# A fixed instruction order for every engine, a spatial product with k outermost, and the middle column inside the odd transform products

## Chip, cores and metric

The kernel runs on one core of one Trainium2 chip. Times are device microseconds (us) from the first to the last instruction of one execution; a kernel's time is the median of its runs.

## The reference

```python
# x: 8 x 3072 x 256, w_in: 256 x 1024, w_spatial: 3072 x 3072, w_out: 512 x 256
X = np.fft.fft(np.fft.fft(x, axis=1), axis=2).real
h = np.maximum(X @ w_in, 0.0)
u, v = h[..., :512], h[..., 512:]
v_n = (v - mean(v)) / np.sqrt(var(v) + 1e-06)            # over the last axis
v_s = np.einsum('ts,bsd->btd', w_spatial, v_n) + b_spatial[None, :, None]
out = (u * v_s) @ w_out
```

The transform over the last axis is folded into `w_in`. The transform over the sequence is done by symmetry: x is added to and subtracted from its reversed copy ("folds"), and the halves are multiplied with cosine and sine tables. Most of the work is the spatial product, 3072 x 3072 by 3072 x 512, eight times (once a batch). In batch 0 the kernel also turns `w_spatial`: 96 pieces are loaded, cast to bf16 by GpSimd, transposed by TensorE, copied out and stored; from batch 1 on the turned weights are loaded again from memory.

Words used below: k numbers the 24 blocks of 128 rows over which one spatial sum runs, and "bank" stands for the PSUM tile of 128 x 512 in which the kernel gathers one such sum. The folds leave two columns without a partner, 0 and 128: their copies are the "edges", and column 128 alone is the "middle column". Four rows of x, one in each quarter, are the "special row" and have a fold of their own. A "settled batch" is one of batches 1 to 6.

## The kernel before

```python
    def turn_w(wt):                                    # batch 0 only, 96 pieces
        wb = wbpool.tile([P, WCOL], BF16, name="wb", tag="wb")       # 2 buffers
        nc.gpsimd.tensor_copy(out=wb, in_=wr)          # or with columns reversed
        load_w()
        pt = psM.tile([P, GK, P], BF16, name="pt", tag="psM")
        for kk in range(GK):
            nc.tensor.transpose(pt[:, kk, :], wb[:, 128 * kk:128 * kk + 128], ident)
        # ... copied to wt by VectorE or ScalarE in turn, and stored

    def dct_class(b, c, gx, sp, eo):                   # c = 0..3
        # ... pe: 3 (c even) or 6 (c odd) products of 384 columns, + the special row
        ops_e += [(xe[:, 0:128], ctx_[:, c, 0:n])]     # 4 rows
        # ... po_: 3 or 6 products, and for odd c the special row again
        nc.scalar.copy(out=view(eo, c, [[4, n]]), in_=pe[:, 0:n])
        nc.vector.tensor_scalar(out=view(eo, EOW + c, [[4, n]]), in0=po_[:, 0:n], ...)

    def dct_128(b, gx, sp, eo):                        # the middle column: one output row
        for c in range(4):
            # ... 3 or 6 products with lhsT of one column, + the special row
        for c in range(4):
            nc.scalar.copy(out=view(eo, EOW + c, [[4, n]])[0:1], in_=pm[32 * c:32 * c + 1, 0:n])

    def spatial(b, c, dt, v, wts, ut):                 # k innermost, two PSUM banks
        pw = psW.tile([P, TC], FP32, name="pw", tag="psW")
        for k in range(KT):
            nc.tensor.matmul(pw, lhsT=v[:, k, 128 * dt:128 * dt + 128],
                             rhs=wts[k // GK][:, k % GK, :], start=(k == 0), stop=(k == KT - 1))
        tm = tpool.tile([P, TC], FP32, name="tm", tag="tm")
        nc.vector.tensor_tensor(out=tm, in0=pw, in1=bbc[:, TC * c:TC * c + TC], op=ALU.add)
        gt = gpool.tile([P, TC], BF16, name="gt", tag="gt")
        nc.vector.tensor_tensor(out=gt, in0=tm, in1=ut, op=ALU.mult)
        return gt

    for b in range(B):                                 # the order is left to the scheduler
        for c in range(NCH):                           # 6 column blocks of 512
            uts = [u_tile(b, c, dt, cur["eo"]) for dt in range(NDT)]
            for dt in range(NDT):
                gts.append(spatial(b, c, dt, cur["v"], wts[c], uts[dt]))
                # ... after dt 0 the projection of the block before; turn_w or loads of
                # weights; one step of the next batch's folds, transform and v
```

## Time and profile before

| | before |
|---|---|
| time, median of the first 3 runs | 1539.09 us (1534.65 to 1540.53) |
| TensorE busy | 1408 us, 91% |
| end of batch 0 (start of its last gate addition) | 374.9 us |
| batches 1 to 6, each, same mark | 168.05 to 169.3 us |
| batch 7, same mark | 145.2 us, and 7 us to the end |

A "gate" is the addition of the bias to a finished spatial sum and the product with u; the last addition of a batch is a mark. The prediction counts with another mark, the first spatial product of batch 1: in before that is 376.6 us, 1.7 after the gate mark. The prediction shows the page's lines on busy engines, slices and waits. First, lines of TensorE's waits in the window from 100 to 400 us (total, times, longest, all in us):

```profile
PE pt L154 <- POOL wb L149: 6.2, 10, 0.8
PE pt L154 <- POOL wb L146: 6.1, 10, 1.3
```

In the kernel before, TensorE's transposes wait 12 us for GpSimd's casts after 100 us, in twenty short waits. Lines of the order of time: start, duration, engine, operation, and in brackets the idle time before it and what ended that.

```profile
126.85 1.23 DVE L308 TENSOR_TENSOR sm<-xt 128x1024 f32<-128x1024 f32 x1 [1.91 <-DMA xt<-xr]
...
151.08 1.23 DVE L308 TENSOR_TENSOR sm<-xt 128x1024 f32<-128x1024 f32 x1 [10.97 <-DMA xt<-xr]
...
156.45 1.89 PE L469 MATMUL pw<-wt,v_t 128*128 128x512 bf16 x4 [15.26 <-ACT v_t L445]
```

VectorE stands in front of batch 1's folds for 1.9 and 11.0 us; the normalised v of batch 0 is behind the second one, and TensorE waits 15.3 us for it.

### The profile page before, as it was taken

What the parts mean: (1) busy time and instruction counts of PE and PEld (TensorE: products, weight loads), DVE (VectorE), ACT (ScalarE), POOL (GpSimd) and SP (SyncE); (2) the same over time, 40 slices, a digit from 0 to 9 for tenths busy, and PEclk for the clock granted to TensorE, in tenths of its full rate; (3) what the DMA queues carried; (4) which work ended last, traced back from release to release, by engine and by line L of the source; (5) the groups of instructions that cost most, each with busy time, mean ns of one, the idle gap of its engine ahead of it and who ended that gap; (6) DMA issues with size and microseconds to landing.
All of it is one profiled execution on the core that took longest, in us unless ns stands there. A gap on an engine that the chain in (4) does not pass through costs nothing.

```text
span 1539.1 us, 18367 instructions
## 1 busy us (share of the span) xinstructions
PE 1408.1 (91%) x7107; PEld 677.9 (44%) x7244; DVE 709.0 (46%) x1466; ACT 479.3 (31%) x806; POOL 143.1 (9%) x202
## 2 busy tenths in 40 slices
PE   1363799999999999999999999999999999999998
PEld 0121444444444444444444444444444444444444
DVE  4755633764247523663248523753256422452222
ACT  3242433444134421342134412432134313341111
POOL 2811342440000000000000000000000000000000
PEclk9566899999999999999999999999999999999999
DMA  7564887884336242453434432633433433324331
GB/s 239 175 244 149 276 292 247 288 302 153 115 123 236 96 181 107 156 200 110 178 129 159 155 132 96 230 139 137 151 124 137 151 128 126 130 106 182 139 149 69
DMA packets 100232, 255.31 MB, mean 166 GB/s; under 512 B 13200, under 2 KB 59824, under 8 KB 100016
## 3 DMA queue, kind: packets, MB, share of 16 engines
q1 hardware_dynamic: 64912, 215.54, 39.6%
q10 hardware_dynamic: 26112, 25.17, 4.6%
q0 software_dynamic: 9120, 13.42, 2.6%
q8 instruction: 56, 0.92, 0.2%
q14 instruction: 32, 0.26, 0.1%
HBM read 210.80 MB, written 56.62 MB: 174 GB/s over the span
## 4 chain that ended last, share of the span: by engine, by line
PE 81%; DMA 8%; DVE 6%; POOL 3%; ACT 1%; issue 1%; SPq 0%; another core or an unknown queue 0%; POOLq 0%; ACTq 0%; DVEq 0%
PE pw L469 59%; PE po L485 5%; DMA xt<-xr 5%; PE pu L461 5%; PE pv L435 4%; PE pm L409 2%; PE pe L386 2%; DMA xr<-in_x_dram 2%; PE pt L154 2%; DVE stt L439 1%; DVE sm L308 1%; DVE xt L310 1%; POOL wb L146 1%; DMA x<-xr 1%; POOL wb L149 1%
## 5 line engine op out<-in xcount | busy, mean ns | idle before, releaser
L469 PE MATMUL pw<-wt,v_t 128*128 128x512 bf16 x4494 | 1023.0, 380 | 40.9 <-ACT v_t L445 35.3
L469 PEld LDWEIGHTS <-v_t 128*128 128x128 bf16 x4608 | 448.5, 98 | 570.3 <-ACT v_t L445 41.4
L473 DVE TENSOR_TENSOR tm<-pw,bbc 128x512 f32<-128x512 f32 x192 | 132.6, 691 | 610.2 <-PE pw L469 610.2
L463 ACT ACTIVATE ut<-pu 128x512 bf16<-128x512 f32 x192 | 101.3, 606 | 186.7 <-PE pu L461 182.3
L476 DVE TENSOR_TENSOR gt<-tm,ut 128x512 bf16<-128x512 f32 x192 | 135.1, 704 | 13.2 <-DVE tm L473 0.5
L439 DVE BATCH_NORM_STATS2 stt<-r 128x6 f32<-128x512 f32 x192 | 125.1, 681 | 29.9 <-ACT r L438 29.8
L489 ACT COPY ot<-po 128x512 f32<-128x512 f32 x96 | 56.2, 585 | 253.8 <-PE po L485 251.0
L438 ACT ACTIVATE r<-pv 128x512 f32<-128x512 f32 x192 | 106.9, 595 | 85.8 <-PE pv L435 73.2
L435 PE MATMUL pv<-weo,eo_t 128*128 128x512 bf16 x278 | 88.6, 394 | 7.0 <-ACT eo_t L413 3.1
L445 ACT ACTIVATE v_t<-r,rs 128x512 bf16<-128x512 f32 x96 | 78.1, 813 | 49.0 <-DVE rs L443 45.9
L485 PE MATMUL po<-wob,gt 128*128 128x256 bf16 x768 | 91.9, 273 | 0.9 <-DVE gt L476 0.9
L461 PE MATMUL pu<-eo_t,weo 128*128 128x512 bf16 x282 | 81.8, 379 | 3.8 <-ACT r L438 2.6
L485 PEld LDWEIGHTS <-gt 128*128 128x128 bf16 x768 | 75.0, 98 | 20.1 <-DVE gt L476 1.2
L388 ACT CAST eo_t<-pe 128x384 bf16<-128x384 f32 (+1 forms) x32 | 32.6, 1019 | 159.3 <-PE pe L386 159.2
L154 PE MATMUL pt<-ident,wb 128*128 128x128 bf16 x576 | 49.1, 230 | 26.9 <-POOL wb L146 17.7
L441 ACT ACTIVATE rs<-mv,epst 128x2 f32<-128x2 f32 x96 | 28.5, 297 | 145.2 <-DVE mv L440 145.1
L159 ACT COPY wt<-pt 128x768 bf16<-128x768 bf16 x48 | 37.8, 800 | 79.3 <-PE pt L154 48.1
L154 PEld LDWEIGHTS <-wb 128*128 128x128 bf16 x576 | 38.0, 103 | 53.2 <-POOL wb L146 25.6
L354 POOL MEMSET xo<- 4x1 bf16 x8 | 0.7, 91 | 618.1 <-PE po__5260 L386 129.7
L435 PEld LDWEIGHTS <-eo_t 128*128 128x128 bf16 x384 | 38.2, 101 | 44.1 <-issue 6.0
L447 DVE TENSOR_SCALAR v_t<-r,mv,rs 128x512 bf16<-128x512 f32 x96 | 54.0, 563 | 0.0
L146 POOL CAST wb<-wr 128x768 bf16<-128x768 f32 x48 | 47.3, 1010 | 70.7 <-PE pt L154 59.9
(206 smaller groups left out, 792.7 us busy)
## 6 DMA issues: line engine op xcount, KB each, us to landing
wt<-wtd SPq DMA_DIRECT2D x168, 768.0 KB, 6.7
wr<-in_moe_w_spatial_dram SPq DMA_DIRECT2D x96, 384.0 KB, 5.0
out_dram<-ot ACTq DMA_DIRECT2D x96, 256.0 KB, 2.1
wtd<-wt SPq DMA_DIRECT2D x24, 768.0 KB, 7.3
xr<-in_x_dram POOLq DMA_DIRECT2D x8, 1536.0 KB, 22.6
xt<-in_x_dram SPq DMA_DIRECT2D x21, 512.0 KB, 8.8
xt<-xr SPq DMA_DIRECT2D x21, 512.0 KB, 5.0
x<-in_x_dram SPq DMA_DIRECT2D x1, 1536.0 KB
```

What stands on the lines that cost most here:

```text
L146: nc.gpsimd.tensor_copy(out=wb, in_=wr)
L154: nc.tensor.transpose(pt[:, kk, :], wb[:, 128 * kk:128 * kk + 128], ident)
L435: nc.tensor.matmul(pv, lhsT=l, rhs=w, start=(kt == 0), stop=(kt == 1))
L438: nc.scalar.activation(out=r, in_=pv, func=AF.Relu)
L439: nc.vector.bn_stats(out=stt[:, jj, :], in_=r)
L445: nc.scalar.activation(out=v[:, 2 * j, :], in_=r2[0], func=AF.Identity, scale=rs[:, 0:1], bias=rs[:, 2:3])
L461: nc.tensor.matmul(pu, lhsT=w, rhs=r, start=(kt == 0), stop=(kt == 1))
L463: nc.scalar.activation(out=ut, in_=pu, func=AF.Relu)
L469: nc.tensor.matmul(pw, lhsT=v[:, k, 128 * dt:128 * dt + 128], rhs=wts[k // GK][:, k % GK, :], start=(k == 0), stop=(k == KT - 1))
L473: nc.vector.tensor_tensor(out=tm, in0=pw, in1=bbc[:, TC * c:TC * c + TC], op=ALU.add)
L476: nc.vector.tensor_tensor(out=gt, in0=tm, in1=ut, op=ALU.mult)
L485: nc.tensor.matmul(po[:, i, :], lhsT=gts[dt][:, t0:t0 + 128], rhs=wob[:, dt, :], start=(dt == 0), stop=(dt == NDT - 1))
```

## The change

Its intent: no scheduler, so that nothing of a later batch can stand in front of what TensorE needs next; four open sums over one group of six k's, so that a weight tile is used up and freed at once; and less transform work, by computing the middle column inside the odd products and adding the special row as a bias while copying out. Cut to its core:

```diff
-NWR = 4
+NWR = 6
+    ctx.enter_context(tc.manual_schedule())
-    wtpool = ... bufs=6        psW = ... bufs=2        psO = ... bufs=2
+    wtpool = ... bufs=5        psW = ... bufs=NDT      # psO gone, projection in psM
     def turn_x(b):             # the reversed copy of x, issued by GpSimd
-        nc.gpsimd.dma_start(...)
+        for q in range(4):
+            nc.gpsimd.dma_start(...)
-    def fold(plus, rev, dst, oe):
+    def fold_even(plus, rev):
+        nc.vector.tensor_tensor(out=sm, in0=plus, in1=rev, op=ALU.add)
+        nc.gpsimd.tensor_copy(out=view(e, 0, [[129, 4], [128, 2]]), in_=...)      # edges
+        # ... five more on VectorE
+    def fold_odd(plus, rev, od, oe):
+        # ... six on oe, and then
+        nc.gpsimd.tensor_copy(out=view(ho, 0, [[P, 2], [1, 1]]), in_=view(od, ...))
     def fold_special(b, xs):   # now wholly on GpSimd
+    def bias_special(xe, xo):  # three products with 4 columns; result is a bias
-    def dct_128(...)
+    def dct_odd(b, c, gx, spb, eo):
+        ops = ops_o[0:1] + ops_m + ops_o[1:]     # ops_m writes row 0 alone
     def v_norm(b, v, pr):
+        eng = nc.gpsimd if b == 0 else nc.vector
+        eng.tensor_scalar(out=v[:, i, :], in0=r2[1], ...)
-    def spatial(b, c, dt, v, wts, ut):           # 24 k's into one bank
+    def spatial(v, wt, pw, g, dt):               # 6 k's into one of four banks
+        for kk in range(GK): ...
+    for ti, (b, c, g) in enumerate(tiles):
+        for dt in range(NDT):
+            spatial(cur["v"], wts[ti], pws[dt], g, dt)
+            if g == NG - 1:
+                gts.append(gate(c, pws[dt], uts[dt]))
+            if ta < len(tiles) and tiles[ta][0] == 0:
+                turn_w(wts[ta])
+            # ... projection halves, u tiles, this step's part of the next batch
```

## The prediction

> **What bounds the kernel now.** I read the page's busy table and slices first, then the PE's list of waits, then the chain of waits, then the order of time on PE inside one settled batch.
>
> ```profile
> PE 1408.1 (91%) x7107; PEld 677.9 (44%) x7244; DVE 709.0 (46%) x1466; ACT 479.3 (31%) x806; POOL 143.1 (9%) x202
> ...
> PE   1363799999999999999999999999999999999998
> ...
> PEclk9566899999999999999999999999999999999999
> ```
>
> TensorE is full from the sixth slice on; what is empty is the first 170 us, at a granted clock of 0.5 to 0.8. Its waits agree: the two longest both belong to the start.
>
> ```profile
> PE pw L469 <- ACT v_t L445: 35.3, 10, 15.3
> PE pw__237 L295 <- DMA scr<-in_moe_w_in_dram: 29.5, 1, 29.5
> ```
>
> Why normalised v came late is in the chain of waits between 100 and 165 us:
>
> ```profile
> 105.74 0.61 DVE eo L319
> ...
> 106.79 19.96 DMA xt<-xr
> 126.85 1.23 DVE sm L308
> ...
> 131.03 19.96 DMA xt<-xr
> 151.08 1.23 DVE sm L308
> ```
>
> The scheduler put batch 1's folds in VectorE's queue among batch 0's normalisation; VectorE is in order, so twice it sat behind a 20 us load that batch 0 doesn't need. This is the largest removable piece.
>
> The settled batches: in VectorE's order of time the first gate additions (L473) of batches 1 and 7, counted off in 24s, start at 381.78 and 1393.50 us; less one 5.18 us spatial product, batch 1 starts at 376.6 and batch 7 at 1388.3. So the kernel is 376.6 + 6 x 168.6 + 150.8. Inside a batch, PE in order of time:
>
> ```profile
> 772.96 0.65 PE L386 MATMUL pe<-ct,ev 128*128 128x384 bf16 x3
> 773.55 0.33 PE L386 MATMUL pe<-ctx__113,xe 4*128 4x384 bf16 x1
> 773.81 0.66 PE L386 MATMUL po__6659<-st,he 128*128 128x384 bf16 x3
> 774.52 5.13 PE L469 MATMUL pw<-wt,v_t 128*128 128x512 bf16 x23
> ```
>
> Starts matter here, not durations: 384 columns every 0.163 us, a 4-row multiplication about 0.1 us dearer than that, nothing idle between.
>
> **What the Trainium skill says.** "TensorE: Matmul & The Clock Gate", section Back-to-back issue gap, gives N/2.4 + 2.5 ns warm: 215.8 ns for 512 columns, 162.5 for 384. The trace agrees (5.18/24 = 0.2158; 0.163). Its section What's actually happening has the clock halved until about 3.4 us of activity; the trace shows multiplications 0.43 us apart at 133 us and 0.21 at 137. "Perfetto Trace Analysis", section Identifying Performance Opportunities, calls a repeating bubble on the engine that should be full a sign of too few buffers; in the settled batches before there is almost none. "SBUF — State Buffer", section Who interferes with whom, says a VectorE operation with two SBUF inputs contends with a GpSimd one that reads SBUF; the odd fold on GpSimd takes 9.7 us beside VectorE the first time and 6.2 the last, so it agrees.
>
> **The change, part by part.**
>
> *Less transform work.* Before, a batch has 42 multiplications of 384 columns for the even and odd products and 22 with one output column (L409). From the chain of waits in a settled batch an even class takes 0.76 + 0.60 us and an odd one 1.24 + 1.35; two of each is 7.9, plus 4.30 for L409: 12.2 us. After, an even class has 3+6, an odd 6+6, together 42, x 0.163 = 6.85; three tiny ones for the special row add about 0.4: 7.3. Saved 4.9 us a batch on the bound engine, before any new wait. It also drops four one-partition copies (4.1 us of ScalarE).
>
> *Floor of a settled batch.* Spatial 576 x 0.2158 = 124.3; u and v 96 x 0.2158 = 20.7; projection 96 x 0.1088 = 10.4; transform 12.2: 167.6, and undisturbed batches measured 168.05, so 0.4 of sundries. After: 124.3 + 20.7 + 10.4 + 7.3 + 0.4 = 163.1.
>
> *What the fixed order puts back.* With k outermost, all four spatial sums of a column block finish within 4 us, and their four gates (addition, then product) come in one burst on VectorE. The groups they and a fold consist of:
>
> ```profile
> L476 DVE TENSOR_TENSOR gt<-tm,ut 128x512 bf16<-128x512 f32 x192 | 135.1, 704 | 13.2 <-DVE tm L473 0.5
> L473 DVE TENSOR_TENSOR tm<-pw,bbc 128x512 f32<-128x512 f32 x192 | 132.6, 691 | 610.2 <-PE pw L469 610.2
> ...
> L308 DVE TENSOR_TENSOR sm<-xt 128x1024 f32<-128x1024 f32 x21 | 26.0, 1236 | 28.3 <-DMA xt<-xr 28.2
> ```
>
> Start to start a dependent pair is 0.79 + 0.65 = 1.44 us. In two of six blocks the order puts a fold between the first gate and the other three: the even fold of piece 1 and the odd fold of piece 2. Take 0 where the first sum ends. First gate done 1.56. Even fold, start to start as at 793 to 796 us: 1.15 + 0.45 waiting for GpSimd's edges + 0.6 + 0.4 + 0.34 + 0.5 = 3.45, so to 5.0; then three gates to 9.3. PE works in groups of six (1.295 us); unhindered it asks for the second bank again after three more groups, a u tile (0.43) and one group of the next block, 5.61, and for the finished products (projection, one group later) at 6.9. It waits 0.15 and then 2.2: 2.4 us. Odd fold: 1.2+0.6+0.34+0.34+0.3+0.3 = 3.1, gates end at 8.95, wait 2.05. Together 4.4 us a batch: nearly the 4.9 saved. I take 163.1 + 4.4 = 167.5.
>
> *The start.* Order on VectorE: three tables, small constants, fold. Each table is 4.6 us plus waiting for ScalarE's cosine (1.5 + 1.56): ready 8.6, then about 28; constants and c2 in strict order, 6.5: fold begins near 34.7, against 35.7 before. (x itself should be there by 30: the reversed copy no longer shares its time with the next one.) GpSimd does three odd folds in 8.5, 7.5 and 7.3 us with seven casts of about 1 us around them: the last ends near 65, the sixth transpose, which PE takes ahead of any transform, near 66.4. Transform at half clock: 42 x 0.32 + 4 x 0.7 = 16.2, + 1: v begins at 83. A v pair in the new order is a chain: relu 0.55, 0.55, then statistics of the second tile 1.2, root 0.35, reciprocal and scale 0.5, normalise 0.81 = 4.0; twelve pairs and six transposed copies in between (0.3 each) = 50, so all v at 134. (In the trace around 137 us the same links stand: relu 0.60, statistics 0.69 and 0.18, root 0.30, reciprocal 0.15, scale 0.21, normalise 0.81.) But PE only needs k 0 to 5 and free banks, and runs about two pairs ahead: the spatial product starts near 127.
>
> *Batch 0.* From there PE owes 124.3 + 10.4 (u) + 8.7 (projection) + 7.3 + 10.4 (v of batch 1) + 480 transposes x 0.057 = 27.4: 188.5. Add 4.4 for the folds, 6 for PE's waits on GpSimd's casts (9.3 us of them lie between 200 and 400 us before), and 6 for the x pieces, because the transfer engines are near their limit then:
>
> ```profile
> core 0: us, PE busy (x) PEld busy (x), PEclk, DMA share, GB/s
> ...
> 175.00:200.00 25.00, 5.71 (x72) 4.36 (x72) 1.00 0.97 333
> ```
>
> That is twelve turned pieces in 25 us, 2.08 each. After, PE could take one every 2.0, so this stretch has no reserve. Batch 0: 205.
>
> *The end.* 124.3 + 9.9 (u) + 10.4 (projection) + 5.8 (gate, last projection, copy, store): 150, as before; no folds in it, so no stalls.
>
> Sum: 127 + 205 + 6 x 167.5 + 150 = 1487 us. The gain, 52, is all in the start (376.6 to 332) but for 7.
>
> **The rivals.** (1) *The gate stalls don't appear* because VectorE chains faster than I add or PE has queued work I overlooked: 163.1 a batch, 6 x 4.4 + 4.4 less: 1456. For it: PE has 46% busy VectorE beside it. Against: bursts, not averages, decide. (2) *Transfers take over.* Batch 0 moves about 52 MB in its first twenty steps (74 pieces of 0.39, 20 stores of 0.79, x and output 6.8); at 333 GB/s that is 155 us against PE's 161. If it runs at 285 as in the later slices before, 182: +21, 1508. In settled batches a piece of x is asked for one step (8.5 us) before VectorE needs it, with a median landing of 8.8; if it came 3 us late, VectorE would hold the gates for that long: +18, 1505. (3) *The start is no faster*, because the fixed order serialises what the scheduler overlapped (v of batch 0 beside spatial product): start + batch 0 at 350: 1505. Against: those two 20 us loads are gone from VectorE's path.
>
> **Range and chances.** The start is uncertain by 10, batch 0 by 12, the settled stalls by 20 to either side; they are independent: about 25. 1452 to 1514. Faster by 2% means under 1508.3; two rivals would have to come together to miss it. Faster 0.86, within 2% 0.13, slower 0.01.
>
> **What would show it.** PE's first spatial product near 127 us and batch 1's near 332; no load of x in the chain between 100 and 130. Transform time 7.3 us a batch without L409's group. In batches 1 to 6, twice a batch, PE waiting about 2 us for a projection's gates, with fold operations between gates on VectorE; if the projection never waits for VectorE, rival 1 holds and a batch is 163. If "xt" loads end VectorE's idle time in the settled batches, or batch 0 exceeds 215 with a transfer share over 0.95, rival 2. The prediction is wrong altogether if settled batches exceed 170 us or batch 0's spatial product starts after 145.

## The result, and the profile after

| | before | after | predicted |
|---|---|---|---|
| time, median | 1538.7 (4 runs) | 1517.8 (1514.8 to 1518.3, 4 runs) | 1487 (1452 to 1514) |
| ratio to before, 95% interval | | 0.9864 (0.984 to 0.9887) | |
| first spatial product of batch 0 | 106.3, then held up | 119.9 | 127 |
| first spatial product of batch 1 | 376.6 | 351.7 | 332 |
| batches 1 to 6, each | 168.0 to 169.3 | 168.5 to 168.7 | 167.5 |
| from the first spatial product of batch 7 | 150.8 | 153.5 | 150 |
| end of batch 0, gate mark | 374.9 | 354.1 | none |

The kernel is 1.4% faster, which is within 2%, and slower than the whole predicted range. The page's busy line and slices of the changed kernel:

```profile
PE 1378.0 (91%) x7092; PEld 670.0 (44%) x7092; DVE 734.9 (48%) x1448; ACT 461.2 (30%) x777; POOL 185.4 (12%) x284
...
PE   1454789999999999999999999999999999999998
...
PEclk9666999999999999999999999999999999999999
```

TensorE is 90% full from the seventh slice on (a slice is 38 us), one later than before, although v of batch 0 was complete sooner (at 128 us, against 178). Lines of its waits from 100 to 400 us, as shown of before:

```profile
PE pt L156 <- POOL wb L148: 24.0, 4, 9.2
PE pt L156 <- POOL wb L151: 8.0, 3, 3.9
```

32 us of waiting for GpSimd's casts after 100 us, where before had 12 and the prediction allowed 6. All of it lies in batch 0. GpSimd's own order of time shows why (its operations on L360 and L328 are the edge copies):

```profile
126.01 2.07 POOL L472 TENSOR_SCALAR v_t<-r,mv,rs 128x512 bf16<-128x512 f32 x1 [2.20 <-DVE rs L466]
128.03 2.91 POOL L98 DMA_DIRECT2D xr<-in_x_dram  x4
130.94 0.83 POOL L148 CAST wb<-wr 128x768 bf16<-128x768 f32 x1
139.63 0.18 POOL L368 CAST xe<-xs 4x2 bf16<-4x2 f32 x1 [7.86 <-DMA xs<-in_x_dram]
...
140.84 2.85 POOL L148 CAST wb<-wr 128x768 bf16<-128x768 f32 x3
...
153.08 0.32 POOL L360 COPY ho<-od 128x2 bf16<-128x2 bf16 x1 [6.36 <-DVE ho L355]
...
183.63 0.32 POOL L360 COPY ho<-od 128x2 bf16<-128x2 bf16 x1 [8.24 <-DVE ho L355]
```

A cast of 0.83 us stands behind seven normalisations of 2.07 us in a row, of which this is the last, and behind four DMA issues (2.91); the next ones stand behind the special row's fold, which waits 7.86 us for its transfer, and later ones behind edge copies, which wait 6.4 and 8.2 us for VectorE's folds. Nothing of this is heavy work: GpSimd is busy 12% of the span. It is one queue, and what TensorE needs next stands last in it. TensorE in order of time over the same stretch:

```profile
131.83 0.82 PE L156 MATMUL pt<-ident,wb 128*128 128x128 bf16 x6 [9.21 <-POOL wb L148]
...
141.71 0.82 PE L156 MATMUL pt<-ident,wb 128*128 128x128 bf16 x6 [6.50 <-POOL wb L148]
142.32 2.77 PE L494 MATMUL pw<-wt,v_t 128*128 128x512 bf16 x6
...
148.24 1.46 PE L494 MATMUL pw<-wt,v_t 128*128 128x512 bf16 x6
```

A wait costs more than its length: behind it six products of the same shape take 2.77 us, and 6 us later 1.46.

In the settled batches the burst of gates that the prediction described is there. VectorE at the end of the first column block of batch 1 (k runs out for all four banks at about 541 to 545 us), then TensorE:

```profile
541.29 0.69 DVE L499 TENSOR_TENSOR tm<-pw,bbc 128x512 f32<-128x512 f32 x1 [9.31 <-PE pw L494]
...
542.74 1.23 DVE L326 TENSOR_TENSOR sm<-xt 128x1024 f32<-128x1024 f32 x1
...
546.26 0.68 DVE L499 TENSOR_TENSOR tm<-pw,bbc 128x512 f32<-128x512 f32 x1
...
549.05 0.68 DVE L499 TENSOR_TENSOR tm<-pw,bbc 128x512 f32<-128x512 f32 x1
```

```profile
549.19 0.28 PE L510 MATMUL po<-wob,gt 128*128 128x256 bf16 x1 [0.52 <-DVE gt L502]
550.59 0.72 PE L510 MATMUL po<-wob,gt 128*128 128x256 bf16 x5 [1.11 <-DVE gt L502]
```

After the first gate a fold comes (542.74 to 546.3), the other three gates follow in a chain of 1.4 us each, and the projection waits twice. Its waits in the six settled batches, 354 to 1365 us:

```profile
PE po L510 <- DVE gt L502: 25.2, 36, 1.1
```

That is six waits and 4.2 us a batch; the prediction had two places a batch.

### The profile page after: what moved, and what is told of

The parts are those of the page before. It is cut to its first block, busy times and chain, and to the rows that moved or that the text cites. A ratio compares the mean times of both kernels' runs of the same rounds, so it can differ in the third digit from the quotient of the medians.

```text
span 1516.5 us, 18163 instructions
## 1 busy us (share of the span) xinstructions
PE 1378.0 (91%) x7092; PEld 670.0 (44%) x7092; DVE 734.9 (48%) x1448; ACT 461.2 (30%) x777; POOL 185.4 (12%) x284
## 4 chain that ended last, share of the span: by engine, by line
PE 70%; DVE 14%; issue 1%; ACT 0%; POOL 0%; DVEq 0%; ACTq 0%; POOLq 0%
PE pw L494 52%; PE po L510 5%; DVE gt L502 5%; DVE tm L499 5%; PE pu L486 4%; PE pv L451 4%; DVE stt L455 2%; PE pe L405 1%; PE pt L156 1%; DVE sm L326 0%; DVE mv L456 0%; DVE xt L346 0%; DVE o L349 0%; DVE e L330 0%; DVE od L335 0%
## 5 line engine op out<-in xcount | busy, mean ns | idle before, releaser
L494 PE MATMUL pw<-wt,v_t 128*128 128x512 bf16 x4608 | 1090.8, 381 | 0.2
L488 ACT ACTIVATE ut<-pu 128x512 bf16<-128x512 f32 x192 | 114.7, 598 | 434.3 <-PE pu L486 429.3
L455 DVE BATCH_NORM_STATS2 stt<-r 128x6 f32<-128x512 f32 x192 | 133.0, 693 | 217.1 <-ACT r L454 216.8
L510 PE MATMUL po<-wob,gt 128*128 128x256 bf16 x768 | 107.2, 275 | 27.8 <-DVE gt L502 27.8
L451 PE MATMUL pv<-weo,eo_t 128*128 128x512 bf16 x288 | 98.2, 400 | 7.6 <-ACT r L454 6.9
L486 PE MATMUL pu<-eo_t,weo 128*128 128x512 bf16 x288 | 94.0, 381 | 2.1 <-ACT r L454 2.1
L159 DVE COPY wt<-pt 128x768 bf16<-128x768 bf16 x45 | 25.0, 555 | 65.6 <-PE pt L156 62.8
L407 ACT ACTIVATE eo_t<-pe,spb 128x384 bf16<-128x384 f32 (+1 forms) x32 | 35.8, 1119 | 63.8 <-PE pe L405 37.1
L326 DVE TENSOR_TENSOR sm<-xt 128x1024 f32<-128x1024 f32 x21 | 27.2, 1293 | 48.6 <-DMA xt<-xr 48.6
L472 DVE TENSOR_SCALAR v_t<-r,mv,rs 128x512 bf16<-128x512 f32 x84 | 46.8, 557 | 0.0
```

What stands on the lines that cost most here:

```text
L451: nc.tensor.matmul(pv, lhsT=l, rhs=w, start=(kt == 0), stop=(kt == 1))
L455: nc.vector.bn_stats(out=stt[:, jj, :], in_=r)
L486: nc.tensor.matmul(pu, lhsT=w, rhs=r, start=(kt == 0), stop=(kt == 1))
L488: nc.scalar.activation(out=ut, in_=pu, func=AF.Relu)
L494: nc.tensor.matmul(pw, lhsT=v[:, k, 128 * dt:128 * dt + 128], rhs=wt[:, kk, :], start=(k == 0), stop=(k == KT - 1))
L510: nc.tensor.matmul(po[:, i, :], lhsT=gts[dt][:, t0:t0 + 128], rhs=wob[:, dt, :], start=(dt == 0), stop=(dt == NDT - 1))
```

## The experiments

Marks are the start of the last gate addition of each batch, as above. After has a before of 1538.7 us in its rounds; of the experiments, the first four have one of 1536.7, the next four of 1535.9 and the last of 1536.8. All results were correct.

| kernel | time, us | ratio to before, 95% interval | end of batch 0 | settled batch |
|---|---|---|---|---|
| after | 1517.8 | 0.9864 (0.984 to 0.9887) | 354.1 | 168.55 |
| a1_small_ops | 1499.8 | 0.9759 (0.9743 to 0.9776) | 335.0 | 168.4 to 170.4 |
| a2_folds_late | 1495.9 | 0.973 (0.9714 to 0.9746) | 349.0 | 165.24 |
| a3_k_inner | 1484.1 | 0.9649 (0.9635 to 0.9664) | 353.2 | 161.63, then 163.12 |
| b1_dct_in_before | 1504.9 | 0.979 (0.9775 to 0.9804) | 373.1 | 163.16 |
| a4_v_on_dve | 1498.5 | 0.9753 (0.9738 to 0.9768) | 333.3 | 168.52 |
| a5_best | 1457.1 | 0.9482 (0.9468 to 0.9497) | 326.8 | 161.63, then 163.12 |
| a6_spec_only | 1508.8 | 0.982 (0.9805 to 0.9834) | 344.1 | 168.52 |
| a8_early_fold | 1519.4 | 0.9886 (0.987 to 0.9903) | 356.1 | 168.52 |
| b3_loads_late | 1524.4 | 0.9914 (0.989 to 0.9938) | 359.7 | 168.0 to 169.0 |

### a1: GpSimd's small operations out of the casts' way

From batch 1 on (so during batch 0 too, which prepares batch 1) the edge copies of the folds go to VectorE, and the special row is folded six steps after its load.

```diff
-        nc.gpsimd.tensor_copy(out=view(e, 0, ...), ...)     # also memset of o, copy into ho
+        oe.tensor_copy(out=view(e, 0, ...), ...)            # oe: GpSimd in batch 0, else VectorE
-        steps[0][0].append(s_spec)                          # load and fold
+        steps[0][0].append(s_xs)                            # load
+        steps[0 if b == 0 else 6][0].append(s_spec)         # fold
```

> The changed kernel, with the folds' small copies of batches 1 to 7 (8 and 2 values a partition) and one memset moved from GpSimd to VectorE, and the special row folded six steps after its load is asked for. Theory A (in batch 0 the big casts stand in GpSimd's order behind small copies that wait for VectorE's folds, and PE's transposes wait for the casts): PE's waits for casts after 100 us fall from 32 to about 10, batch 1 starts near 333 instead of 353.9, time about 1497. Rival B (transfers set batch 0's pace): batch 1 still starts at 350 or later, time within 5 us of 1518. A settled batch stays at 168.6 or gains up to 0.6, for VectorE has a little more to do.

Measured: 1499.8 us, batch 0 shorter by 19.1. Lines of TensorE's waits from 119.85 to 335 us:

```profile
PE pt L156 <- POOL wb L148: 9.2, 1, 9.2
...
PE pt L156 <- POOL wb L151: 0.2, 1, 0.2
```

32.0 us of waiting became 9.4, and only the wait behind the normalisations and issues is left. The last normalisation of v and the first spatial product started when they did in after (126.0 and 119.9 us), so the gain lies behind them, in the casts. It is less than the 22.6 us of waiting that went, because TensorE has about 7 us of new waits, for VectorE's copies of turned weights and its gates. That the transfers held batch 0 in after falls: with GpSimd out of the way they simply ran faster, at 0.95 of the engines' time between 142 and 184 us (0.76 in after). Four settled batches are 0.8 to 1.8 us longer; in the trace TensorE there waits up to 1.9 us for gates (4.5 us over batches 1 to 5; after has no such wait), the edges now being in VectorE's queue.

### a2: the folds behind the burst

```diff
-            steps[3 * a][0].append(lambda a=a: s_even(a))
-            steps[3 * a + 1][0].append(lambda a=a: s_odd(a))
+            steps[3 * a][3 if a == 1 else 0].append(lambda a=a: s_even(a))
+            steps[3 * a + 1][3 if a == 2 else 0].append(lambda a=a: s_odd(a))
```

> The changed kernel, with the two folds that stand between gates put after the fourth gate of their step. Theory A (those folds make PE wait 2.3 and 1.1 us a batch, and the bare burst of gates 0.5): a settled batch falls from 168.55 to about 166.2, all seven together 16 us, time about 1502. Rival B (the wait only moves: the late odd fold keeps the transform waiting, or the next step's work stands behind it): a settled batch stays above 168, time above 1513.

Measured: 165.24 us a batch, 3.3 less, and 1495.9 us: somewhat more than expected. The waits of the projection over the six settled batches:

```profile
PE po L510 <- DVE gt L502: 9.6, 18, 0.8
```

Batch 0 ended 5.1 us sooner too, which the expectation did not count; 1.4 of that precede the first spatial product (see a6). So the two folds between gates cost 3.3 us a batch, against the 4.4 of the prediction, and 18 of the 36 waits are left without any fold in the way: four gates in a row are themselves a burst.

### a3: k innermost from batch 1 on

The settled batches finish one sum after another again, everything else of the change stays. Seven weight buffers are needed for that, and room for them comes from NWR 4.

```diff
-            spatial(cur["v"], wts[ti], pws[dt], g, dt)
-            if g == NG - 1:
-                gts.append(gate(c, pws[dt], uts[dt]))
+            if b == 0:                                    # as in after
+                ...
+            else:
+                spatial(cur["v"], wts[ti - g + dt], pws[g], dt, g)
+                if dt == NG - 1:
+                    gts.append(gate(c, pws[g], uts[g]))
```

> The changed kernel, with k innermost (one sum after another) in batches 1 to 7, seven weight tiles and four raw pieces instead of five and six; batch 0 keeps k outermost. Theory A (k outermost brings the four gates of a block in one burst, and that costs 5.5 us a batch): a settled batch falls from 168.55 to about 163.3, and time by 31 to 35 us to about 1485. Rival B (k innermost needs a block's four tiles at once and waits for loads, or the gates matter little): a settled batch stays above 167, time above 1508.

Measured: 163.12 us in five of six settled batches (161.63 in the first, whose opening mark is still one of a burst), and 1484.1 us. TensorE's whole list of waits from 353.2 to 1330.4 us is one, at the border of batch 0:

```profile
PE po L510 <- DVE gt L502: 0.8, 1, 0.8
```

This is the predicted floor of 163.1. K outermost costs 5.4 us in each settled batch. The run also changes the number of buffers, but that is not needed to explain it: counted from start to start of TensorE's operations in after, against the spacing that the same operations have in a3, the time lost at gates makes 5.4 us in one settled batch (batch 3), which is the whole difference. Batch 0 ended at 353.2, so four raw pieces and seven weight buffers make less than a microsecond there.

### b1: the transform part alone, in the kernel before

The scheduler, two banks and k innermost stay; `dct_class` and `dct_128` give way to `bias_special`, `dct_even` and `dct_odd`.

```diff
-            dct_class(b, c, st_["gx"], st_["sp"], st_["eo"])
+                st_["spb"] = bias_special(*st_["sp"])
+            dct_even(b, c, st_["gx"], st_["spb"], st_["eo"])
+            dct_odd(b, c, st_["gx"], st_["spb"], st_["eo"])
-        steps.append(s_128)
```

> The kernel before with only the transform of the change: the middle column inside the odd products, the special row as a bias; order left to the scheduler. Theory A (PE sets the pace and this part alone is worth 4.9 us a batch, the rest of the change having given it back in the settled batches): a settled batch falls from 168.6 to about 163.7, time by 33 to 39 us to about 1502. Rival B (the bias adds a wait, or PE's work was not what bound): a settled batch above 167, time above 1525.

Measured: 163.16 us a settled batch and 1504.9 us, faster than the full change. The transform part is worth some 5.4 us a batch (168.6 to 163.2; predicted 4.9). Batch 0 ends nearly as in before (373.1 and 374.9). So the change as a whole gains 5.4 us a batch by one part and gives 5.4 back by another.

### a4: the normalisation of v on VectorE

```diff
-        eng = nc.gpsimd if b == 0 else nc.vector
+        eng = nc.vector
```

> After, with the normalisation of v of batch 0's odd tiles on VectorE and not on GpSimd (nothing else). Theory A, GpSimd's queue: each of its twelve normalisations costs GpSimd about 2.1 us and stands in the chain of a v pair; on VectorE one costs about 0.55, so the spacing of the v pairs goes from 4.28 to about 3.7 us, v is done some 7 us sooner, and the 9.2 us wait of PE for the first cast of reversed weights shrinks. VectorE gets 6 us of work in the start, which it has room for. Batch 0 ends at about 341 (354 in after), time about 1504. Theory B, the start is paced by ScalarE's or VectorE's own part of the pair: the spacing stays above 4.1, time 1513 to 1518. Settled batches unchanged at 168.5 under both.

Measured: 1498.5 us; batch 0 ends at 333.3, 8 us sooner than I expected. One normalisation takes 0.54 us instead of 2.07. The pairs come every 3.9 us (3.7 expected, 4.28 in after), v is done at 121.2 instead of 128.1. The first spatial product starts 5.2 us sooner than in after (1.5 of that may be the start's clock, see a6); the other 15.6 us are in the casts and what hangs on them. The first wait of TensorE, 9.21 us at 131.83 in after:

```profile
123.37 0.82 PE L156 MATMUL pt<-ident,wb 128*128 128x128 bf16 x6 [3.10 <-POOL wb L148]
```

Its waits for casts after 100 us sum to 19.0 us (32.0 in after).

### a6: only the special row's fold later

The last edit of a1 alone.

> After, with only this: the special row is loaded where it was, but its fold stands six steps later, so that GpSimd's queue no longer waits for that transfer (7.9 us of waiting at 139.6 us in after). Theory A, GpSimd's queue: PE's second wait for a cast (6.5 us) goes, batch 0 is 5 to 8 us shorter, time 1510 to 1513. If the queue is held by something else at that place (the fold's edge copy, which waits for VectorE at 140.7), the wait only changes its name: time 1516 to 1518. Settled batches 168.5 under both, perhaps less by a few tenths.

Measured: 1508.8 us, batch 0 shorter by 10.0, a little better than expected. TensorE's second and third wait:

```profile
133.99 0.51 PE L156 MATMUL pt<-ident,wb 128*128 128x128 bf16 x6 [0.33 <-POOL wb L148]
144.00 0.82 PE L156 MATMUL pt<-ident,wb 128*128 128x128 bf16 x6 [2.88 <-POOL wb L148]
```

The 6.5 us wait is 0.33, and 2.9 us come back later. Of the 10.0, 1.5 lie before the first spatial product, where this edit changes nothing: the granted clock between 45 and 60 us was 1.00 in this profiled run and in those of a2 and a4, and 0.50 in that of after. The runs of after are of other rounds: by the medians the whole gain is 9.0 us, by the ratios to before 6.8. So a1's 19.1 us seem to be half the special row and half the edge copies, which wait for VectorE's folds.

### a8: an early fold put back on purpose

```diff
+    first = prep(1)
+    early = first[1][0][0].pop(1)          # the first even fold of batch 1
         for f in part: f()
+        if i == 13:                        # among the v of batch 0; its load is at step 12
+            early()
```

> After, with the first even fold of batch 1 put into VectorE's order among the normalisation of v of batch 0, its x load issued one step before: the flaw that I read in the kernel before, done on purpose. Theory: an in-order VectorE stands at that fold until the load has landed, and v behind it. The load was 20 us in before, where many transfers ran; here, with fewer at that time, 6 to 12. The v pairs then come 6 to 12 us later, and the spatial product of batch 0 starts later by that: 1523 to 1530. Part is given back because this fold is then missing from batch 0 behind it (3 us). Rival: the load is hidden there because VectorE is not the link that paces v: within 3 us of after, 1515 to 1520, and my reading of the start of before is not what made it late.

Measured: 1519.4 us, 1.6 more than after, so the rival's number. But it does not test what I meant it to test: in the trace the load had landed when VectorE came to the fold at 81.5 us (no idle time before it), so no stall was made. It only shows that the fold's own 3.5 us there cost about 2. The test had to be made in the kernel before.

### b3: the early folds taken out of the kernel before

```diff
+        if after is not None:              # batch 1 only: one number of batch 0's last v
+            nc.vector.tensor_copy(out=xt[0:1, 0, 0:1], in_=after)
         nc.sync.dma_start(out=xt[:, 0:4, :], ...)
```

> The kernel before, with one thing: each x load of batch 1 must first see one number of batch 0's last normalised v (a copy of a single element into its tile), so the scheduler can no longer put batch 1's folds among that normalisation. Theory (prediction's reading of before): VectorE's waits for those loads, 1.9 us at 126.9 and 11.0 us at 151.1, hold v, and PE's 15.3 us wait at 156 hangs on the second; without them v is done 12 to 20 us sooner and the kernel takes 1522 to 1530. Rival: another thing takes over at once, because the folds that are moved must still be done during batch 0, each now behind a load that starts later, with VectorE standing still in front of the turned weights that PE needs: 1533 to 1545. Settled batches unchanged, 168 to 169 us each.

Measured: 1524.4 us, 12.4 less than before, in the expected range; batch 0 ends 15.2 us sooner. Batch 0's last v is started at 157.2 us (177.0 in before). TensorE's longest wait for v is 2.5 us in place of 15.3 (90 to 200 us):

```profile
PE pw L471 <- ACT v_t L447: 16.4, 9, 2.5
```

So the reading of before's start was right in kind, and is worth 12 us of time. (The profiled run of before was a slow one among its fast runs, 1540.8 us against a median of 1539.1, so marks taken from it may flatter a comparison by 1 or 2 us.)

### a5: everything together

All edits of a1, a4 and a3, and the reversed copy of x issued two groups later. No single run isolates that last edit.

```diff
-            if b + 2 < B:                  # at c == 0, g == 0
+        if c == 0 and g == 2 and b + 2 < B:
                 xrs[b + 2] = turn_x(b + 2)
```

> After, with everything together that the readings so far speak for: the small copies of the folds on the idle engine VectorE from batch 1 on, the special row's fold six steps behind its load, the normalisation of v all on VectorE, the reversed pieces of x issued a little later, and k innermost from batch 1 on with seven buffers for the turned weights. If the losses are separate (GpSimd's queue in batch 0; bursts of gates in the settled batches), the gains add: batch 0 ends at 322 to 332, settled batches 163.1, end 145: 1447 to 1456; allowing for a rest of waits 1465. If they share a cause (one hides behind the other once it is gone, for example transfers in batch 0 taking over), batch 0 stays at 335 or above and the time is 1460 to 1475. Either way it should beat both kernels.

Measured: 1457.1 us (1455.4 to 1458.3), 5.2% faster than before and 4.0% faster than after by the medians. Batch 0 ends at 326.8. Busy time by engine from there to the start of the last gate addition (length, then TensorE, its weight loads, VectorE, ScalarE, GpSimd, with instructions; granted clock, transfer share, GB/s):

```profile
core 0: us, PE busy (x) PEld busy (x) DVE busy (x) ACT busy (x) POOL busy (x), PEclk, DMA share, GB/s
326.79:1449.00 1122.21, 1121.39 (x5589) 542.76 (x5587) 549.89 (x1151) 326.94 (x565) 15.90 (x32) 1.00 0.44 154
```

TensorE is busy 1121.4 of 1122.2 us at full clock: nothing is left there but its own work. The gains of a1 (19.1 us of batch 0) and a4 (20.8) do not add, the two together with the later issue make 27.3: they empty the same queue.

## Why the prediction was wrong, point by point

**The sum.** At the prediction's own marks, 1487 missed 19.7 us in start and batch 0 (332 predicted, 351.7 measured), 6.3 in the settled batches (168.55 each, for 167.5) and 3.5 at the end. That gives the trace's span of 1516.5; a run's time is 1.8 us more than its span, and the median lies 0.5 below the profiled run.

**What failed: batch 0, the term "6 for PE's waits on GpSimd's casts".** It measured 32.0. The spatial product started at 119.9, not 127, so 7 us were won there; from then to the first spatial product of batch 1 it took 231.8 us, not 205. Of these 27 us more, 26 are this term. That the rest is nearly nothing is luck, for three other terms missed and cancel. The trace gives them, if each of TensorE's starts is counted to the next against the undisturbed spacing (0.2158 us for 512 columns, 0.163 for 384, 0.1088 for 256, 0.057 for a transposition): own work 188.2 (188.5 predicted), waits 32.4, and 11.2 of wider spacing, most of it in the tens of microseconds that have the waits. So products at a lower clock behind the waits (2.77 us instead of 1.46 for six), which were not in the sum at all, cost up to 11; the waits for gates came to 0.3 instead of 4.4, and no wait of TensorE shows the 6 put in for the x pieces.

The term was wrong because of how it was found: I took the cast waits of before between 200 and 400 us and scaled them, although the change moves the special row's fold and the last edge copy to GpSimd and fixes their place. GpSimd's order in the changed kernel (normalisations, four issues, one cast, special row, edge copy, casts) could have been read before any run. Runs a1, a4 and a6 each take occupants out of that queue: the waits for casts fall from 32.0 to 9.4, 19.0 and 25.8, and batch 0, counted from its first spatial product to the gate mark, from 234.3 us to 215.1, 218.7 and 225.7. This cause is shown.

**The start.** Right in kind, and the number was better than predicted by two errors of opposite sign. The first product for v came at 74 us, not 83: the transform took about 11 us, not 17, partly at full clock. A pair of v took 4.28 us, not 4.0: the sum overlooked that every second normalisation goes to GpSimd, at 2.07 us (on VectorE, 0.54, a pair takes 3.9, a4). Together v was complete at 128 us (134 predicted). That "twice it sat behind a 20 us load" was overstated, VectorE stood 1.9 and 11.0 us; b3 puts the flaw at 12.4 us of the whole time. The figure of 20 did not enter the sum. The clock "of 0.5 to 0.8" in the first 170 us leaves out the first slice, which the prediction's own line shows at 0.9.

**Less transform work, and the floor.** Right: 5.4 us a batch (4.9 predicted) and a floor of 163.12 (163.1), in b1 and a3.

**The fixed order's stalls.** Right in mechanism, too small: 4.4 predicted, 5.4 measured. The places were partly wrong. I had put 2.4 and 2.05 us in two blocks and nothing in the others. In the trace, start to start, the first boundary between blocks costs 2.2 us, the second 1.1, the one between batches 1.0, and two more 0.55 each; a2 takes the folds away and 2.1 us a batch stay. The four gates alone, 1.4 us each in a row, are enough to make the projection wait.

**The end.** 153.5 measured from batch 7's first spatial product, 150 predicted. The sum's projection term, 10.4, is one batch's; here the last block of batch 6 is projected after the mark too, which makes 112 x 0.1088 = 12.2. "No stalls" was also wrong: a3, without bursts, needs 152.2 for this stretch, so 1.3 are waits for gates.

**The rivals.** Rival 1 (no stalls) fell with a3. Rival 2 (transfers take over) fell with a1; the sign that I had named, batch 0 over 215 us with a share over 0.95, was half there: 232 us, but 0.76 and 0.88 from 142 to 210 us, and at most 0.92, from 250 to 300 us, where TensorE was busy throughout. Rival 3 had nearly the right number for start and batch 0 together (350), for a reason that did not hold: the start was faster. The rival that came true, an engine busy 12% of the span whose queue is in the wrong order, was not on my list, and so the range of 12 us given to batch 0 was too narrow.

**Where the gain went.** Of the 52 us predicted, the start and batch 0 brought 21 and lost more than that to GpSimd's queue (48 in a5, both at the gate mark); in the settled batches 32 us were won by the transform and 32 given back by k outermost.

What stays open: of the 209 us that a5's batch 0 still takes from its first spatial product to that of batch 1, 188.2 are own work, 12.2 waits (only 3.1 of them for casts) and 8.5 wider spacing, and no run removes those last two. With a transfer share of 0.94 between 142 and 184 us, transfers may be next; that is not shown. Nor is what the later issue of x is worth by itself.

## What to carry to other kernels

When an order is fixed by hand, read the queue of every engine, the idle ones above all: what an engine does in a microsecond can hold the bound engine for nine if it stands behind something that waits. Put what waits for transfers or for other engines behind what the bound engine needs next, and give each such operation to an engine whose queue can bear the wait. And test the parts of a many-sided change one by one: here one part alone beat the whole, because another took back exactly what it gave.

## What the Trainium skill lacked or had wrong

- "GPSIMD Engine Reference", section Engine selection, calls one-input operations on GpSimd "roughly line-rate". The casts agree: 0.82 us for 128x768, 1.07 ns a column, where VectorE's normalisation (below) takes 1.05. The subtraction and multiplication with two per-partition scalars does not: 2.07 us for 128x512, where VectorE took 0.54 for the same instruction. The page has no figure for this form.
- "TensorE: Matmul & The Clock Gate", section Back-to-back issue gap: the prediction uses its N/2.4 + 2.5 ns, which the page gives for an isolated multiplication; for a stream with weight loads the page has about 131 ns at 512 columns. Here 24 in a stream, each with its own weight load, took 5.18 us, 215.8 ns each: the formula held, the lower figure did not.
- "Perfetto Trace Analysis", section Matmuls, advises that independent groups rotate through PSUM banks, so that evacuating one overlaps the next group. It does not say that interleaving the groups over k makes them end together: four open banks cost 5.4 us in a batch of 163.1, against one sum after another in the same four banks (a3).
- No page that I read gives the price of small operations that stand in one engine's queue ahead of another's input: 26 us more waiting than predicted here, with GpSimd busy 12% of the span.
